# Attention of the first batch pair in whole 128-wide tiles, output stores at another place, and the last addition of the second channel weight's rounding in an adding DMA

## The chip, the core and the metric

The kernel runs on one core of a Trainium2 chip. TensorE (PE) multiplies, VectorE (DVE) and ScalarE (ACT) do elementwise work, GpSimd (POOL) does some too, SyncE (SP) issues most DMAs. The metric is device time in microseconds, lower is better.

## The reference

All inputs are float32 in value; the four MLP weights come in as 8-byte numbers (double precision) and are rounded to float32 on the chip.

```python
kv  = einsum('bhsd,bhse->bhde', k, v)          # 8 batches, 8 heads, s=576, d=64
out = einsum('bhsd,bhde->bhse', q, kv)         # linear attention, no softmax
out = out / sqrt(mean(out*out, -1) + 1e-6) * g_norm
x   = heads side by side                       # (8, 576, 512)
h   = relu(x^T @ w_tok1) @ w_tok2              # token mixing, 576 -> 256 -> 576
u   = x + h^T
out = u + relu(u @ w_ch1) @ w_ch2              # channel mixing, 512 -> 1536 -> 512
```

## The kernel before, in words

A "pair" is two batches (its two "sides"); there are four pairs. The first 200 us are the **front**: attention and token mixing of the pairs, woven with the rounding of the weights. Then comes **channel mixing** for nine groups of 512 rows (eight batches, and the 64 left-over rows of each batch as a ninth), with two nested levels of a seven-product scheme, fed by sums that DVE makes.

The order of the front is written out by hand as lists of step names (`start`, `middle`, `steady`, `last`), which `play` calls one after another. Every instruction is kept in that order on its engine, so a list fixes the order of work on each engine and in each DMA queue. The names: `kvSH` the k^T v products of side S, half H of the heads (into a `ps_kv` bank), `eSH` their copy to `kvp`, `lSH` the load of later k and v, `lqS` the load of q; `aC` the attention product of chunk C (two tiles of 128 rows; chunk 4 is the left-over rows of both sides), `gCh`, `qCh`, `tCh` gain (DVE, L392), square (ACT, L396) and sum of squares (DVE, L412) of one PSUM bank of it, `mC rC iC` mean, square root and a refined reciprocal (L417 to L431), `sCT` and `pCT` the scaling of tile T by ACT (L438, eight small instructions) or by POOL (L443, one instruction). Then `hST` are the first token products, `hr` their remainder with the relu, `uI` the second ones for tile I of nine, `zI` a copy of x into the PSUM bank that `uI` adds to ("seeded" tiles, read back by ACT; the others are added to x by DVE). `jN` are N matmuls of the identity in a stretch with nothing to multiply. `wNK` is step K of rounding token weight block N, `fN` a fetch, a bare number that many further steps of the channel weights' rounding.

Rounding a block (`decode`) is one ACT instruction and then six on DVE: `clamp`, `shift`, `sign`, `power`, `lower`, `both` (in the profile L163, L166, L170, L174, L183, L187, and L118 for `both`, which adds `part` to the block). `part` has one buffer. The second channel weight has six blocks of 128x1024 elements (512 KB each), rounded in the last pair's attention and after it. The first sums of channel mixing read them (`d<-w_ch`, L118).

PSUM in the front: two banks tagged "o" (attention), two "kv", four "h" (token mixing). In `attend` the PE is split into four 64x64 parts; a chunk takes both "o" banks, heads of even number in one and of odd number in the other:

```python
matmul(o[h][ds(n * HF, HF), t, hp],
       lhsT=qT[2 * pair + side][r, hp, ds((2 * (c % 2) + t) * P + n * HF, HF)],
       rhs=kvp[side][r, hp], start=True, stop=True)
```

At the end of the last group, `outer` adds four partial results straight onto the output tile (`put_on`, `write`, `take`, all L118), `xadd` adds the rest, and `store` and `store_rest` (L115) write the 64-row pieces out, half on SP's queue and half on ACT's. The helpers record everything at a few lines: L115 DMA, L118 DVE add, L121 relu, L124 ACT copy, L127 matmul.

Of the kernel before, what the change touches and what calls it, by code (L numbers as in the profile page):

```python
# [19 lines left out]
def kernel(  # L20
# [81 lines left out]
    v_in = [inp.tile([P, JJ, DH], F32, name=f"v_in{i}") for i in range(4)]  # L102
    kvp = [inp.tile([P, HP, D], F32, name=f"kvp{i}") for i in range(2)]
    u_dram = [dram.tile([J * P, DM], F32, name=f"u_dram{g}") for g in range(NG)]
# [43 lines left out]

    def decode(dst, raw):

# [39 lines left out]
        def both():  # L190
            tensor_add(dst, dst, part[0])

# [8 lines left out]

    def block(n, loads, dst):
# [12 lines left out]
        return (fetch,) + decode(dst, turn)  # L215

# [18 lines left out]
    def get_ch2(f):  # L235

        a = 2 * (2 * f // NS)

        def loads(raw):
            t = raw.rearrange("p (h f n) w -> p f h n w", h=2, f=2)  # L240
            rows = words(moe_w_ch2)[ts(f, 2 * P)].rearrange("(f p) (h n) w -> f p h n w", f=2, h=2)
            return [(t[:, i], rows[i]) for i in range(2)]

        dst = w_ch2[:, a:a + 2, ds(2 * f % NS, 2)]
        return block(2 * DM, loads, dst.rearrange("p h f n -> p h (f n)"))

# [84 lines left out]
    def attention(pair, groups):  # L331


        bank, stat, kv_ps = {}, {}, {}

        def kv(side, half):
            n = 4 * pair + 2 * side + half
            kk, vv = k_in[n % 4], v_in[n % 4]

            o = kv_ps[side, half] = ps["kv"].tile([P, 2, D], F32, name="ps_kv")  # L340
            for i in range(2):
                for j in range(JJ):
                    for h in range(2):
                        at = ds(i * P + h * D, D)
                        matmul(o[ds(h * D, D), i], lhsT=kk[:, j, at], rhs=vv[:, j, at],
                               start=(j == 0), stop=(j == JJ - 1), skip_group_check=True)

        def evict(side, half):
            o = kvp[side][:, 2 * half:2 * half + 2]
            if pair == 0:  # L350
                keep(nc.vector.tensor_copy(o, kv_ps[side, half]))
            else:
                copy(o, kv_ps[side, half])

        def attend(c):
            o = [ps["o"].tile([P, 2, HP, D], F32, name="ps_o", tag="o") for _ in range(2)]
            side = c // 2
            for t in range(2):  # L360
                for hp in range(HP):
                    for n in range(2):
                        for h in range(2):
                            r = ds(h * D, D)
                            matmul(o[h][ds(n * HF, HF), t, hp],
                                   lhsT=qT[2 * pair + side][r, hp, ds((2 * (c % 2) + t) * P + n * HF, HF)],
                                   rhs=kvp[side][r, hp], start=True, stop=True)
            for h in range(2):
                bank[c, h] = o[h].rearrange("p t k d -> p (t k) d")

        def attend_rem():
            o = [ps["o"].tile([P, HP, D], F32, name="ps_r", tag="o") for _ in range(2)]
            for hp in range(HP):
                for side in range(2):
                    for h in range(2):
                        r = ds(h * D, D)
                        matmul(o[h][ds(side * HF, HF), hp], lhsT=qT[2 * pair + side][r, hp, LO:],
                               rhs=kvp[side][r, hp], start=True, stop=True)
            for h in range(2):
                bank[4, h] = o[h]  # L380


        number = lambda c: HP if c == 4 else 2 * HP
        sq = {}

        def gain(c, h):
            if (pair, c) not in X:
                n = 1 if c == 4 else 2
                X[pair, c] = xps[pair % 2].tile([P, n, DM], F32, name="x", tag=f"x{n}",
                                                bufs=4 if n == 2 else 1)  # L390
            x = X[pair, c].rearrange("p t (k h d) -> p (t k) h d", h=2, d=D)[:, :, h]
            keep(nc.vector.tensor_mul(x, bank[c, h], g_sb.to_broadcast([P, number(c), D])))  # L392
# [8 lines left out]
        def stats_of(c):  # L401

            g = group(c)
            at = sum(2 * number(i) for i in g if i < c)
            return [t[:, ds(at, 2 * number(c))].rearrange("p (h k) o -> p h k o", h=2) for t in stat[g]]

        def total(c, h):
            g = group(c)
            if g not in stat:
                stat[g] = [stats.tile([P, sum(2 * number(i) for i in g), 1], F32, name=name)  # L410
                           for name in ("ms", "root", "inv")]
# [12 lines left out]
        def invert(g):  # L424
# [6 lines left out]
            keep(nc.vector.reciprocal(inv, root))  # L431

        def scale(c, t):
            x = X[pair, c][:, t].rearrange("p (k h d) -> p k h d", h=2, d=D)
            inv = stats_of(c)[2][:, :, ts(t, HP)]
            for k in range(HP):
                for h in range(2):
                    keep(nc.scalar.activation(x[:, k, h], x[:, k, h], AF.Copy, scale=inv[:, h, k]))  # L438

        def scale_pool(c, t):  # L440
            x = X[pair, c][:, t].rearrange("p (k h d) -> p k h d", h=2, d=D)
            inv = stats_of(c)[2][:, :, ts(t, HP)].rearrange("p h k o -> p k h o")
            keep(nc.gpsimd.tensor_mul(x, x, inv.to_broadcast([P, HP, 2, D])))  # L443

# [6 lines left out]
        for c in range(5):  # L451
            steps[f"a{c}"] = do(attend, c) if c < 4 else attend_rem
            for h in range(2):
                steps |= {f"{n}{c}{h}": do(f, c, h) for n, f in zip("gqt", (gain, square, total))}
# [6 lines left out]

    def token_mixing(pair, seeds):
        h1, acc = {}, {}
# [25 lines left out]
        def tok2(i):  # L489
            if i not in seeds:  # L490
                acc[i] = ps["h"].tile([P, DM], F32, name="ps_u", tag="h")
            first = i not in seeds
# [229 lines left out]
    def outer(place, size, mul, to, base=None, act=copy, onto=False):  # L722
# [56 lines left out]
        at(2, "c", False, True, lambda: take(0, 0, "c", act))  # L779
        put(place + PLACE[7] + 2, do(put_on, 1, 1, "u3"), do(write, 1, 1, "b", "u3"))  # L780
        at(4, "a", False, True, lambda: take(1, 0, "a", copy) if onto else read(to(1, 0), 1, 0))
# [79 lines left out]
    def channel2(g, n0):  # L861
# [104 lines left out]
        else:  # L966
            for place, steps in ((40, [xadd(1, 0, 4)]), (43, [xadd(0, 1, 6)]), (44, [radd(7, 6)]),
                                 (46, [xadd(1, 0, 7)]), (47, [xadd(1, 1, 7)]), (49, [xadd(0, 1, 5)]),
                                 (50, [xadd(1, 1, 5), do(store, g, xg, 1)]),
                                 (52, [do(store_rest, xg, 1)]), (56, [do(store_rest, xg, 0)])):  # L970
# [70 lines left out]
    for t in [t for pair in zip(k_in, v_in) for t in pair]:  # L1041
        keep(nc.gpsimd.memset(t[HF:, J], 0.0))

    root = stats.tile([P, 1], F32, name="root")
# [9 lines left out]
    for block in tok1[2:] + tok2:  # L1054
# [13 lines left out]
    middle = [  # L1068
# [6 lines left out]
    def steady(n0, n1):  # L1075
        return [
            "kv00 l00 e00 1 -s40", "h00 3", "kv01 l01 e01 1", "h01 3", f"a0 q00 g01 q01 g00 {n0}",
# [3 lines left out]
            "u6 t30 t31 m2 r2 1 i2 p20 p21 s30", f"u7 1 s31 {n1}", "u8 2"]  # L1081

    attentions = [attention(0, ((0,), (1,), (2,), (3,), (4,)))]
    attentions += [attention(p, ((0, 1), (2, 3, 4))) for p in range(1, B // 2)]
    mixings = [token_mixing(p, (2, 4, 6) if p < B // 2 - 1 else range(2, 9)) for p in range(B // 2)]
    more = {f"w{n}{k}": f for n, b in enumerate(tok1 + tok2) for k, f in enumerate(b)}
# [13 lines left out]
    for n in range(1, B // 2 - 1):  # L1100
        play(steady(*((2, 0), (2, 1))[n - 1]), attention=attentions[n + 1], mixing=mixings[n], before=attentions[n],
             rounding=rounding)
# [15 lines left out]
    def turn(i):  # L1118
# [6 lines left out]
    last = [  # L1125
        "h00 c0 2 -s40 2", "h01 c1 2", "h10 c2 2", "h11 c3 2", "hr 1", "u0 z2 1", "u1 z3 1", "u2 z4",
        "u3 z5 1", "u4 z6 1", "u5 z7 1", "u6 z8 1", "u7 c4", "u8"]
    more = {f"c{i}": do(turn, i) for i in range(J)}
# [95 lines left out]
```

## Time and profile before

| what | us |
|---|---|
| median of three runs (813.44 to 814.81) | 813.64 |
| the profiled execution: its own time | 815.8 |
| span of its profile | 813.9 |
| PE busy in the span | 786.6 (97%) |
| DVE busy in the span | 681.5 (84%) |
| POOL busy in the span | 77.0 (9%) |

The profiled execution took 2.2 us more than the median of the runs and 1.9 us more than its own span. Busy time is the time in which an engine worked on an instruction. In lists of instructions a line gives start, duration, engine, line, operation, "written <- read", shape, count, and in brackets how long the engine idled before it and what it waited for. One float32 matmul shows as two records on PE.

### The profile page before, as it was taken

The page shows a single profiled execution, that of the slowest core. Times are in us where ns is not written, and L with a number is a line of the kernel's source. Part 1 is how long each engine was busy: PE and PEld are TensorE (multiplying, and loading weights), DVE is VectorE, ACT ScalarE, POOL GpSimd, SP SyncE. Part 2 cuts the span into 40 slices and gives each one's busy share as a digit, 9 for nine tenths or more (in the row PEclk, how much of TensorE's full clock was granted, in tenths as well). Part 3 has the DMA queues.
Part 4 walks back from the last instruction along what each step waited for, and adds up shares of the span by engine and source line. Part 5 has one row for each costly group of instructions (what it writes and reads, how often), then busy time and mean ns, then how long its engine had stood idle before and what let it go on. Part 6 is the DMA issues. An engine that isn't in the chain of part 4 may idle for free.

```text
span 813.9 us, 18057 instructions
## 1 busy us (share of the span) xinstructions
PE 786.6 (97%) x7204; PEld 689.5 (85%) x7204; DVE 681.5 (84%) x1308; ACT 308.1 (38%) x863; POOL 77.0 (9%) x72
## 2 busy tenths in 40 slices
PE   5799999999999999999999999999999999999996
PEld 5445555443788899999999999999999999999996
DVE  3577999999786978987997997897898899799686
ACT  1466667583220034243234233333424323423431
POOL 1100101010000011003003003001100200300300
PEclk9999999999999999999999999999999999999998
DMA  9999999336458567468658638737836855764542
GB/s 286 293 337 294 358 360 347 130 129 178 151 200 274 198 203 242 144 207 233 198 172 255 212 123 279 236 118 230 283 125 213 259 166 196 235 195 147 195 142 82
DMA packets 97348, 175.54 MB, mean 216 GB/s; under 512 B 7024, under 2 KB 54128, under 8 KB 97264
## 3 DMA queue, kind: packets, MB, share of 16 engines
q1 hardware_dynamic: 95584, 172.65, 65.3%
q10 hardware_dynamic: 1680, 1.74, 0.7%
q8 instruction: 57, 0.93, 0.5%
q14 instruction: 27, 0.22, 0.1%
HBM read 137.79 MB, written 36.57 MB: 214 GB/s over the span
## 4 chain that ended last, share of the span: by engine, by line
PE 84%; DVE 8%; DMA 4%; ACT 3%; issue 1%; ACTq 0%; DVEq 0%
PE ps_a L127 37%; PE ps_b L127 18%; PE ps_c L127 9%; PE ps_v L127 4%; PE ps_w L127 4%; PE ps_h L127 4%; PE ps_u L127 4%; ACT x L438 2%; DMA qT<-in_q_dram 1%; DMA v_in<-in_v_dram 1%; PE ps_o L127 1%; DMA k_in<-in_k_dram 1%; DVE ms L412 1%; DVE x L392 1%; PE ps_kv L127 1%
## 5 line engine op out<-in xcount | busy, mean ns | idle before, releaser
L124 ACT COPY u<-ps_a 128x128 f32<-128x128 f32 (+1 forms) x160 | 56.2, 351 | 156.6 <-PE ps_a L127 156.6
L118 POOL TENSOR_TENSOR v<-v,v 128x384 f32<-128x384 f32 (+1 forms) x48 | 61.4, 1300 | 534.4 <-ACT v L124 494.6
L127 PE MATMUL ps_b<-uT,sums 128*128 128x128 f32 x672 | 86.2, 276 | 0.0
L127 PEld LDWEIGHTS ps_b<-uT,sums 128*128 128x128 f32 x672 | 80.7, 192 | 0.2
L118 DVE TENSOR_TENSOR v<-v,v 128x768 f32<-128x768 f32 (+1 forms) x86 | 79.4, 930 | 1.1
L127 PE MATMUL ps_a<-uT,w_ch 128*128 128x128 f32 x576 | 78.8, 275 | 0.0
L124 ACT COPY ps_c<-ps_a 128x128 f32<-128x128 f32 (+1 forms) x80 | 27.0, 337 | 129.5 <-PE ps_a L127 129.5
L127 PE MATMUL ps_u<-h,w_tok 128*128 128x512 f32 (+1 forms) x160 | 69.7, 620 | 3.8 <-DVE w_tok L118 1.9
L118 DVE TENSOR_TENSOR v<-ps_b,u 128x384 f32<-128x384 f32 x112 | 61.3, 547 | 12.7 <-PE ps_b L127 10.8
L127 PEld LDWEIGHTS ps_a<-uT,w_ch 128*128 128x128 f32 x576 | 71.5, 192 | 0.4
L127 PE MATMUL ps_h<-x,w_tok 128*128 128x512 f32 (+1 forms) x160 | 67.3, 612 | 1.5 <-POOL x L443 1.5
L118 DVE TENSOR_TENSOR uT<-uT 128x512 f32<-128x512 f32 (+4 forms) x103 | 63.0, 627 | 0.8
L127 PE MATMUL ps_a<-uT,w 128*128 128x128 f32 x432 | 60.0, 275 | 0.0
L438 ACT ACTIVATE x<-x,inv 128x64 f32<-128x64 f32 x208 | 52.2, 338 | 11.3 <-DVE inv L431 11.3
L127 PEld LDWEIGHTS ps_u<-h,w_tok 128*128 128x128 f32 (+1 forms) x160 | 25.1, 183 | 35.1 <-issue 27.2
L127 PEld LDWEIGHTS ps_a<-uT,w 128*128 128x128 f32 x432 | 54.0, 192 | 0.0
L127 PEld LDWEIGHTS ps_h<-x,w_tok 128*128 128x128 f32 (+1 forms) x160 | 26.0, 190 | 32.3 <-issue 27.2
L121 ACT ACTIVATE v<-v 128x384 f32<-128x384 f32 (+1 forms) x86 | 42.5, 529 | 22.9 <-DVE v L118 22.5
L118 DVE TENSOR_TENSOR xg<-xg,r 128x512 f32<-128x512 f32 x74 | 49.9, 684 | 0.6
L118 DVE TENSOR_TENSOR sv<-v 128x384 f32<-128x384 f32 x80 | 43.3, 550 | 8.0 <-ACT v L121 8.0
L127 PE MATMUL ps_a<-sums,sv 128*128 128x128 f32 x336 | 47.0, 276 | 0.0
L127 PE MATMUL ps_a<-uT,sums 128*128 128x128 f32 x336 | 46.8, 276 | 0.0
(133 smaller groups left out, 1560.2 us busy)
## 6 DMA issues: line engine op xcount, KB each, us to landing
sums<-sums SPq DMA_DIRECT2D x112, 576.0 KB, 4.0
qT<-in_q_dram SPq DMA_DIRECT2D x8, 1152.0 KB, 9.4
xt<-u_dram SPq DMA_DIRECT2D x36, 256.0 KB, 3.7
blocks<-y SPq DMA_DIRECT2D x72, 128.0 KB, 2.6
uT<-blocks SPq DMA_DIRECT2D x36, 256.0 KB, 4.7
xg<-u_dram SPq DMA_DIRECT2D x18, 512.0 KB, 4.8
k_in<-in_k_dram SPq DMA_DIRECT2D x16, 512.0 KB, 9.4
u_dram<-x SPq DMA_DIRECT2D x16, 512.0 KB, 4.9
```

The costliest lines, as they stand in the source:

```text
L118: keep(engine.tensor_tensor(out=o, in0=a, in1=b, op=op))
L121: keep(nc.scalar.activation(o, a, AF.Relu))
L124: keep(nc.scalar.copy(o, a))
L127: keep(nc.tensor.matmul(*a, **kw))
L392: keep(nc.vector.tensor_mul(x, bank[c, h], g_sb.to_broadcast([P, number(c), D])))
L412: keep(nc.vector.tensor_reduce(stats_of(c)[0][:, h], sq[c, h], axis=AX.X, op=ALU.add))
L438: keep(nc.scalar.activation(x[:, k, h], x[:, k, h], AF.Copy, scale=inv[:, h, k]))
```

## The change

1. For pair 0 only (`whole`), the two "kv" banks are zeroed once by DVE and the k^T v products go to the diagonal 64x64 blocks of 128x128 squares. `attend_tile` then multiplies a whole tile of 128 rows by such a square: four 128x128 matmuls per tile in place of 16 of 64x64, into one "o" bank per tile instead of two per chunk. `e` copies 128x256 elements instead of 128x128; gain, square and sum work on one tile each; the left-over rows take one bank. The list `start` is rewritten for it: the tiles `p00 p01 p11 p20 p21 p30 p31` are scaled by POOL and `s10 s40` by ACT (before, ACT scaled one tile of every chunk), `kv11` stands ahead of `h000`, and `j6` and `j2` are added.
2. `both` of the second channel weight's six blocks becomes an accumulating DMA issued by POOL (`part` added to the block in SBUF, 512 KB).
3. In the steady pairs (pairs 2 and 3 of the attention) some scalings are recorded after the matmul or the copy they stood ahead of, and the bare numbers change: three and one more rounding steps in the first of them where there were two and none, none in the second where there were two and one.
4. In the last token mixing, `u0` and `u1` get the "o" banks (free by then), and each seed `z` comes one step earlier.
5. In the last product of the last group, `put_on`/`write` of one quarter come one place earlier; `xadd(1,1,5)` and the store of two pieces move from place 50 to 48, `xadd(0,1,5)` from 49 to 50.

The core of the diff (other hunks only carry `by_dma`, `whole` and the wider `kvp` through):

```diff
...
-    kvp = [inp.tile([P, HP, D], F32, name=f"kvp{i}") for i in range(2)]
+    kvp = [inp.tile([P, HP, P], F32, name=f"kvp{i}") for i in range(2)]
...
         def both():
-            tensor_add(dst, dst, part[0])
+            if by_dma:
+                keep(nc.gpsimd.dma_start(dst, part[0], accum_op=ALU.add))
+            else:
+                tensor_add(dst, dst, part[0])
...
-        return block(2 * DM, loads, dst.rearrange("p h f n -> p h (f n)"))
+        return block(2 * DM, loads, dst.rearrange("p h f n -> p h (f n)"), by_dma=True)
...
+        whole = pair == 0
...
-            o = kv_ps[side, half] = ps["kv"].tile([P, 2, D], F32, name="ps_kv")
+            if whole:
+                o = kv_ps[side, half] = zeroed[half]
+            else:
+                o = kv_ps[side, half] = ps["kv"].tile([P, 2, P], F32, name="ps_kv", tag="kv")
             for i in range(2):
                 for j in range(JJ):
                     for h in range(2):
                         at = ds(i * P + h * D, D)
-                        matmul(o[ds(h * D, D), i], lhsT=kk[:, j, at], rhs=vv[:, j, at],
+                        matmul(o[ds(h * D, D), i, ds(h * D if whole else 0, D)], lhsT=kk[:, j, at],
+                               rhs=vv[:, j, at],
                                start=(j == 0), stop=(j == JJ - 1), skip_group_check=True)
...
-            o = kvp[side][:, 2 * half:2 * half + 2]
-            if pair == 0:
-                keep(nc.vector.tensor_copy(o, kv_ps[side, half]))
+            n = P if whole else D
+            o, i = kvp[side][:, 2 * half:2 * half + 2, :n], kv_ps[side, half][:, :, :n]
+            if whole:
+                keep(nc.vector.tensor_copy(o, i))
             else:
-                copy(o, kv_ps[side, half])
...
+                copy(o, i)
+
+        def attend_tile(c, t):
+            side = c // 2
+            o = ps["o"].tile([P, DM], F32, name="ps_o", tag="o")
+            bank[c, t] = o.rearrange("p (h d) -> p h d", d=D)
+            for hp in range(HP):
+                matmul(o[:, ts(hp, P)], lhsT=qT[2 * pair + side][:, hp, ts(2 * (c % 2) + t, P)],
+                       rhs=kvp[side][:, hp], start=True, stop=True)
+
+        def attend_tile_rem():
+            o = ps["o"].tile([P, DM], F32, name="ps_r", tag="o")
+            bank[4, 0] = o.rearrange("p (h d) -> p h d", d=D)
+            for hp in range(HP):
+                for side in range(2):
+                    matmul(o[ds(side * HF, HF), ts(hp, P)],
+                           lhsT=qT[2 * pair + side][:, hp, LO:],
+                           rhs=kvp[side][:, hp], start=True, stop=True)
...
-                                   rhs=kvp[side][r, hp], start=True, stop=True)
+                                   rhs=kvp[side][r, hp, :D], start=True, stop=True)
...
+        number = lambda c: HP if c == 4 and not whole else H
+        parts = lambda c: 1 if c == 4 and whole else 2
...
-            x = X[pair, c].rearrange("p t (k h d) -> p (t k) h d", h=2, d=D)[:, :, h]
+            if whole:
+                x = X[pair, c][:, h].rearrange("p (h d) -> p h d", d=D)
+            else:
+                x = X[pair, c].rearrange("p t (k h d) -> p (t k) h d", h=2, d=D)[:, :, h]
...
+        def inv_of(c, t):
+
+            inv = stats_of(c)[2]
+            if whole:
+                return inv[:, t].rearrange("p (k h) o -> p k h o", h=2)
+            return inv[:, :, ts(t, HP)].rearrange("p h k o -> p k h o")
...
             x = X[pair, c][:, t].rearrange("p (k h d) -> p k h d", h=2, d=D)
-            inv = stats_of(c)[2][:, :, ts(t, HP)].rearrange("p h k o -> p k h o")
-            keep(nc.gpsimd.tensor_mul(x, x, inv.to_broadcast([P, HP, 2, D])))
+            keep(nc.gpsimd.tensor_mul(x, x, inv_of(c, t).to_broadcast([P, HP, 2, D])))
...
-            steps[f"a{c}"] = do(attend, c) if c < 4 else attend_rem
-            for h in range(2):
+            if whole:
+                steps |= {f"a{c}{t}": do(attend_tile, c, t) if c < 4 else attend_tile_rem
+                          for t in range(parts(c))}
+            else:
+                steps[f"a{c}"] = do(attend, c) if c < 4 else attend_rem
+            for h in range(parts(c)):
                 steps |= {f"{n}{c}{h}": do(f, c, h) for n, f in zip("gqt", (gain, square, total))}
...
             if i not in seeds:
-                acc[i] = ps["h"].tile([P, DM], F32, name="ps_u", tag="h")
+                n = "o" if i in aside else "h"
+                acc[i] = ps[n].tile([P, DM], F32, name="ps_u", tag=n)
...
-        put(place + PLACE[7] + 2, do(put_on, 1, 1, "u3"), do(write, 1, 1, "b", "u3"))
+        put(place + PLACE[7] + (1 if onto else 2), do(put_on, 1, 1, "u3"), do(write, 1, 1, "b", "u3"))
...
         else:
             for place, steps in ((40, [xadd(1, 0, 4)]), (43, [xadd(0, 1, 6)]), (44, [radd(7, 6)]),
-                                 (46, [xadd(1, 0, 7)]), (47, [xadd(1, 1, 7)]), (49, [xadd(0, 1, 5)]),
-                                 (50, [xadd(1, 1, 5), do(store, g, xg, 1)]),
+                                 (46, [xadd(1, 0, 7)]), (47, [xadd(1, 1, 7)]), (48, [xadd(1, 1, 5), do(store, g, xg, 1)]),
+                                 (50, [xadd(0, 1, 5)]),
                                  (52, [do(store_rest, xg, 1)]), (56, [do(store_rest, xg, 0)])):
...
+    zeroed = [ps["kv"].tile([P, 2, P], F32, name="ps_kv", tag="kv") for _ in range(2)]
+    for t in zeroed:
+        keep(nc.vector.memset(t, 0.0))
...
     start = [
         "kv00 e00 l00 j14 w01 w11 w02 w03 w04 w05 w06 w07 w12 w13 w14 w15 w16 w17", "kv01 j10 e01 l01 f0",
-        "a0 q00 g01 q01 g00 t00 t01 m0 r0", "a1 g11 q10 i0 g10 q11 p00 s01 t10 t11 m1 r1",
-        "kv10 e10 i1 p10 s11", "h000 h001", "kv11 e11", "h002 h003",
-        "a2 q20 g21 q21 g20 t20 t21 m2 r2", "h010 h011", "a3 g31 q30 i2 g30 q31 p20 s21 t30 t31 m3 r3",
-        "h012", "a4 i3 p30 s31 q40 g41 q41 g40 t40 t41 m4 r4", "h013 w21 i4 s40 lq0 l10 l11"]
+        "a00 g00 q00", "a01 g01 q01 t00", "a10 g10 q10 t01 m0 r0", "a11 g11 q11 t10 i0 p00 p01",
+        "kv10 j6 t11 m1 r1 e10 i1 s10 p11", "kv11 j2 e11", "h000 h001 h002 h003", "a20 g20 q20", "a21 g21 q21 t20",
+        "h010 t21 m2 r2", "a30 g30 q30 i2 p20", "a31 g31 q31 t30", "h011 t31 m3 r3 p21", "a40 i3 p30 g40 q40 p31",
+        "h012 h013 t40 m4 r4 w21 i4 s40 lq0 l10 l11"]
...
-            "u0 i0 1", "kv11 l11 e11", "u1 1 s00", "u2 z4 1", "a2 q20 g21 q21 g20 s01", "u3 t20 t21",
-            "u4 1 z6", "a4 q40 g41 q41 g40 lq0 s10", "u5 t40 t41 1", "a3 q30 g31 q31 g30 lq1 s11",
-            "u6 t30 t31 m2 r2 1 i2 p20 p21 s30", f"u7 1 s31 {n1}", "u8 2"]
+            "u0 i0 1", "kv11 l11 e11", "u1 1 s00", "u2 z4 1", "a2 q20 g21 q21 g20", "u3 s01 t20 t21",
+            "u4 z6 1", "a4 q40 g41 q41 g40 lq0", "u5 s10 t40 t41 1", "a3 q30 g31 q31 g30 lq1",
+            "u6 s11 t30 t31 m2 r2 1 i2 p20 p21 s30", f"u7 1 s31 {n1}", "u8 2"]
...
-    mixings = [token_mixing(p, (2, 4, 6) if p < B // 2 - 1 else range(2, 9)) for p in range(B // 2)]
+
+    mixings = [token_mixing(p, (2, 4, 6)) for p in range(B // 2 - 1)]
+    mixings.append(token_mixing(B // 2 - 1, range(2, 9), (0, 1)))
...
-        play(steady(*((2, 0), (2, 1))[n - 1]), attention=attentions[n + 1], mixing=mixings[n], before=attentions[n],
+        play(steady(*((3, 1), (0, 0))[n - 1]), attention=attentions[n + 1], mixing=mixings[n], before=attentions[n],
...
-        "h00 c0 2 -s40 2", "h01 c1 2", "h10 c2 2", "h11 c3 2", "hr 1", "u0 z2 1", "u1 z3 1", "u2 z4",
-        "u3 z5 1", "u4 z6 1", "u5 z7 1", "u6 z8 1", "u7 c4", "u8"]
+        "h00 c0 2 -s40 2", "h01 c1 2", "h10 c2 2", "h11 c3 2", "hr z2 1", "u0 z3 1", "u1 z4 1", "u2 z5",
+        "u3 z6 1", "u4 z7 1", "u5 z8 1", "u6 1", "u7 c4", "u8"]
```

More of the change, by code (lines that the diff above doesn't have):

```diff
@@ L146, in load_q, with decode @@
             dma(qT[b], q[b].rearrange("(c p) s -> p c s", p=P))
-    def decode(dst, raw):
+    def decode(dst, raw, by_dma=False):
         bits = dst.bitcast(U32)
@@ L200, in like, with block @@
         return flat if len(dst.shape) == 2 else flat.rearrange("p (a n) -> p a n", a=dst.shape[1])
-    def block(n, loads, dst):
+    def block(n, loads, dst, by_dma=False):
         raw = []
@@ L213, in turn @@
             return t if len(dst.shape) == 2 else t.rearrange("p (a n) w -> p a n w", a=dst.shape[1])
-        return (fetch,) + decode(dst, turn)
+        return (fetch,) + decode(dst, turn, by_dma)
     def get_tok1(t):
@@ L377, in attend_rem @@
                         matmul(o[h][ds(side * HF, HF), hp], lhsT=qT[2 * pair + side][r, hp, LO:],
-                               rhs=kvp[side][r, hp], start=True, stop=True)
+                               rhs=kvp[side][r, hp, :D], start=True, stop=True)
             for h in range(2):
                 bank[4, h] = o[h]
-        number = lambda c: HP if c == 4 else 2 * HP
+        number = lambda c: HP if c == 4 and not whole else H
+        parts = lambda c: 1 if c == 4 and whole else 2
         sq = {}
@@ L403, in stats_of @@
             g = group(c)
-            at = sum(2 * number(i) for i in g if i < c)
-            return [t[:, ds(at, 2 * number(c))].rearrange("p (h k) o -> p h k o", h=2) for t in stat[g]]
+            n = lambda i: parts(i) * number(i)
+            at = sum(n(i) for i in g if i < c)
+            return [t[:, ds(at, n(c))].rearrange("p (h k) o -> p h k o", h=parts(c)) for t in stat[g]]
         def total(c, h):
@@ L409, in total @@
             if g not in stat:
-                stat[g] = [stats.tile([P, sum(2 * number(i) for i in g), 1], F32, name=name)
+                stat[g] = [stats.tile([P, sum(parts(i) * number(i) for i in g), 1], F32, name=name)
                            for name in ("ms", "root", "inv")]
@@ L431, in invert @@
             keep(nc.vector.reciprocal(inv, root))
+        def inv_of(c, t):
[3 more added lines that the diff above has]
+            return inv[:, :, ts(t, HP)].rearrange("p h k o -> p k h o")
         def scale(c, t):
             x = X[pair, c][:, t].rearrange("p (k h d) -> p k h d", h=2, d=D)
-            inv = stats_of(c)[2][:, :, ts(t, HP)]
+            inv = inv_of(c, t)
             for k in range(HP):
                 for h in range(2):
-                    keep(nc.scalar.activation(x[:, k, h], x[:, k, h], AF.Copy, scale=inv[:, h, k]))
+                    keep(nc.scalar.activation(x[:, k, h], x[:, k, h], AF.Copy, scale=inv[:, k, h]))
         def scale_pool(c, t):
             x = X[pair, c][:, t].rearrange("p (k h d) -> p k h d", h=2, d=D)
-            inv = stats_of(c)[2][:, :, ts(t, HP)].rearrange("p h k o -> p k h o")
-            keep(nc.gpsimd.tensor_mul(x, x, inv.to_broadcast([P, HP, 2, D])))
+            keep(nc.gpsimd.tensor_mul(x, x, inv_of(c, t).to_broadcast([P, HP, 2, D])))
         steps = {}
@@ L459, in attention, with token_mixing @@
         return steps
-    def token_mixing(pair, seeds):
+    def token_mixing(pair, seeds, aside=()):
         h1, acc = {}, {}
```

## The prediction

> **What bounds the kernel now.** I read the busy time by stage first, then the chain of work that ended last, then PE's own list for its gaps. By stage (columns: stretch, length, busy time and count of PE, PE's weight loads, DVE, ACT, POOL, then granted clock, DMA share, GB/s):
>
> ```profile
> 31.00:59.00 28.00, 23.22 (x339) 12.68 (x340) 18.90 (x46) 14.09 (x43) 2.12 (x2) 0.93 1.07 323
> 85.00:128.00 43.00, 42.74 (x527) 22.15 (x523) 39.64 (x69) 28.92 (x88) 2.79 (x2) 1.00 1.07 363
> 128.00:173.50 45.50, 43.56 (x530) 22.25 (x526) 43.53 (x67) 29.78 (x87) 2.79 (x2) 1.00 0.54 197
> 206.60:805.00 598.40, 598.40 (x5025) 588.64 (x5026) 508.84 (x1009) 190.73 (x523) 61.39 (x48) 1.00 0.61 199
> ```
>
> From 206.6 to 805 PE has no gap, so no edit can gain there; a gain has to be made in the front or the last 9 us, and every us that PE starts 206.6 sooner is a us off the end. The chain (start, length, what) shows what holds the front:
>
> ```profile
> 19.64 11.20 DMA qT<-in_q_dram
> ...
> 35.25 2.86 issue
> ...
> 48.12 2.03 ACT x L438 x8
> ...
> 58.66 4.52 PE ps_u L127 x6
> ...
> 206.59 36.46 PE ps_v L127 x168
> ```
>
> Up to 30.84 DMA sets the pace, then pair 0's second half runs through small DVE and ACT steps with a 2.86 us PE wait that no semaphore explains, then the rounding of w_tok2 ends at 58.5 and lets `u0` go. PE's gaps:
>
> ```profile
> 38.11 0.30 PE L127 MATMUL ps_o<-kvp,qT 64*64 64x64 f32 x2 [2.86 <-issue]
> 58.66 4.51 PE L127 MATMUL ps_u<-h,w_tok 128*128 128x512 f32 x6 [1.92 <-DVE w_tok L118]
> ...
> 160.88 1.98 PE L127 MATMUL ps_u<-h,w_tok 128*128 128x512 f32 x4 [0.74 <-ACT ps_u L124]
> 166.91 1.16 PE L127 MATMUL ps_o<-kvp,qT 64*64 64x64 f32 x64 [1.12 <-ACT sq L396]
> 197.58 9.00 PE L127 MATMUL ps_u<-h,w_tok 128*128 128x512 f32 x24 [1.10 <-ACT ps_u L124]
> ```
>
> The tail, DVE's last rows and the store:
>
> ```profile
> 806.53 0.29 DVE L118 TENSOR_TENSOR xg<-ps_b,xg 128x128 f32<-128x128 f32 x1
> ...
> 807.92 0.29 DVE L118 TENSOR_TENSOR xg<-ps_b,xg 128x128 f32<-128x128 f32 x1
> ```
>
> **What the Trainium skill says.** (1) "DMA: Bandwidth & Descriptors", section "SWDGE vs HWDGE vs iDMA": accumulating is possible only in DMAs issued from GpSimd, whose descriptors a program on GpSimd writes; "Anatomy of one DMA — SWDGE (gpsimd) path" prices one at 2.0 us + bytes / 436e3. No such DMA is in this trace. (2) "SBUF — State Buffer", section "Who interferes with whom": a DVE instruction in a two-port mode locks GpSimd out, descriptor writing included. The trace has contention of that kind: an L118 `w_ch` add of 128x768, else 0.96 us, took 1.70 us where POOL was scaling. (3) "Runtime: NRT & Kernel Launch", section "Instruction fetch mechanics": instructions come in blocks of 256 by a DMA, mostly hidden. The 2.86 us "issue" gap, in the middle of 64 tiny records while the DMA engines are full, looks like one that wasn't; the trace doesn't name it.
>
> **1, pair 0 by whole tiles.** PE: a tile is 4 matmuls = 8 records; 12 records of 128x128 take 1.34 us, so 0.89 us, and a chunk 1.8 instead of 1.16. Nine tiles cost 8.0 us for about 6.2; PE has gaps here, so this 1.8 costs little. `e`: a 128x256 PSUM read takes 0.42 for 0.28, four times +0.14, hidden before 30 us. What it gives is that a gain starts after one tile and an "o" bank returns when its tile is read.
>
> I laid the new list out by hand with the row durations: gain and sum 0.63, square 0.60, `m` 0.17, root 0.22, `i` 0.87, POOL scale 1.06, `h` 0.95, kv 1.31. The first tile starts at 18.4 as before; `i0` ends at 25.2 and POOL has x0 at 26.3 (before 25.4), x1 at 27.3. `kv11` now stands ahead of `h000` and needs v that was issued at 16.2 to 18.7 and lands 9 to 10 us later, about 27; so `h003` ends at 32.5 and `a20` runs then, not at 30.97. That is 1.5 us given away. From there: tiles 32.5 to 34.3, `t21` to 36.3, `i2` to 38.0, `t31` 39.9, `i3` 41.2, `g40` 41.8, `t40` 43.1, `i4` 44.4. Before, `i4` ended at 48.09. The w_tok2 rounding behind it takes 10.5 us (48.0 to 58.5), so it ends at 54.9. PE meanwhile: `kv00` 40.6, `h10` (x7 scaled by POOL at 43.4) to 45.5, `kv01` (its v lands about 44.5) to 46.9, `h11`, `hr`, `a0` to 53.6, first half of `u0` 54.5. So `u0` goes on at 54.9 for 58.66: **-3.7 us**. The 2.86 gap goes with it: 104 fewer matmuls for the same work ask for instructions more slowly. If the gap recurs elsewhere, the gain is about 1.5; if `kv11` doesn't wait, 5.2. Later loads are no bar: q of the next pair lands at 49.4 (issued 41.75, 7.6 to landing) and is needed at 52.5; k and v needed at 61.6 were issued by 50.3 and land within 10 us.
>
> **2, the adding DMA.** It takes six DVE adds of 1.22 us off, 7.3 in all, three in pair 3 and three after. It adds six DMAs in POOL's queue: behind them wait POOL's `p20 p21` of pair 3 only, needed 10 us later. The new wait is DVE's: `power` of the next block writes the one `part` and waits for the DMA. Everything of DVE stands behind it. Latency L: at least 2.0 + 524288/436e3 = 3.2 (estimate from page 1); 512 KB weight loads at that place took 4.5 to landing, plus 1.4 of `clamp` and `shift` (0.68 + 0.69) that may keep POOL from writing descriptors: I take **L = 6**; upper end 9, as the k and v loads in full DMA traffic (9.4).
>
> Block 0 to 1 in pair 3 is the tight place: only 2.6 us of `clamp`, `shift`, `sign` between. From the gain of `a0` (138.98): 1.28 + power 0.69 + sums 1.27 + `lower` 1.21 = 143.4; + 6 = 149.4; power, `lower` 1.92: the gain of `a1` starts at 151.3 for 152.24. Two further steps now lie ahead (1.9 us, edit 3); DVE's waits in pair 2 (0.19 + 0.69 + 0.92 + 0.57) take most, say 0.6 is left. Net +0.3 us of the 0.74 gap; at L = 3.2 both gaps there go (+1.9), at L = 9 -2.3. The next blocks have over 7 us between. After pair 3, block 4 to 5 has 3.9 us, so 2.1 of stall, but three adds are gone (3.7): nothing. The first `d<-w_ch` that needs block 5 has 6.9 us.
>
> **3, moved scalings.** On ACT they keep their place but for one copy that now precedes `s10`/`s11`; order on PE is unchanged. The added step in pair 2 brings an ACT rounding read ahead of the relu of `hr`; its load, issued at 96.07, lands at 104.5, so the relus end 1.3 us later, and squares behind them about 0.5. **+0.4 us** lost (0 to 1.5).
>
> **4, u0 and u1 in "o".** The 1.10 gap at 197.58 is ACT's seed waiting for a DVE add (196.25) to free an "h" bank. Those banks are no longer taken: **-1.1 us**. Next late is uT's sums (in before at 204.96; first needed 1.8 us into ps_v): not late.
>
> **5, tail.** The last product waits 0.24 us for the `write` at 806.53; that comes at 805.96. DVE's last add then ends near 807.8 for 808.21. Each queue issues its four stores one after another from 807.45, 2.47 us in SP's queue and 2.75 in ACT's, so the fourth starts near 809.4; with the first two gone at 805.8 it starts at 808.0. **-1.3 us** (0.4 if only PE's gap counts, 1.5).
>
> Sum: 3.7 + 0.3 - 0.4 + 1.1 + 1.3 = 6.0. The profiled execution's 815.8 becomes 809.8; against the median, 813.64 - 6.0 = **807.6**.
>
> **Rivals.** (A) The start is held by DMA or by another instruction gap: part 1 gives 1.0, sum 3.3, 810.3. For it: DMA share 1.07 from 24 to 140. Against: no PE wait for DMA after 30.84. (B) No `kv11` wait and a short L: 5.2 + 1.5 - 0.4 + 1.1 + 1.3 = 8.7, 804.9. (C) The other side: the adding DMA is slow. Beyond L = 6 pair 3 loses 1 us per us; from 8.6 uT's sums lose it again. At L = 12: pair 3 -4.9, later -3.4, sum 3.7 - 0.4 - 4.9 - 3.4 + 1.1 + 1.3 = -2.6, 816.2; it decides from L about 10.7. For it: L is in no row here, and a two-port lock can hold POOL. Against: DMA share is only 0.54 there. (D) What is gained is absorbed by a later wait of the front, such as ACT's squares at 166.9: 813.
>
> **How the numbers follow.** Chances: forecast (805.8 to 809.4) 0.53, A 0.18, B 0.15, C 0.08, D 0.06. Range 803.8 to 811.8. A difference under 0.2%, 1.6 us, can't be told from none. Faster by more: 0.53 + 0.15 + most of A, 0.85; within 0.08; slower 0.07.
>
> **What would show it.** Right: `u0` of pair 0 complete near 55; no "issue" gap at 35; `power` in pair 3 waiting for a POOL DMA some 3 us once; the PE gap at 197 gone; the last stores issued by 808.7. Wrong: `kv11` or `kv01` waiting for v longer than here, a `part` wait over 6 us, or new gaps in PE between 60 and 200.

## The result, and the profile after

The changed kernel takes as long as the kernel before: 814.54 us (median of four runs, 813.81 to 814.89) against 814.11 (four runs, 813.44 to 814.81); ratio 1.0004, 95% interval 0.9987 to 1.0021. The forecast was 807.6 us.

The change did most of what it was forecast to do, and gave it all back in one place. The same stages as shown of before, in the profile of the changed kernel (same columns; this execution took 813.81 us, the least of its four, and its span is 812.0, 1.9 us less than that of before, though the medians agree):

```profile
31.00:59.00 28.00, 27.27 (x300) 15.62 (x299) 23.07 (x51) 12.69 (x30) 4.08 (x4) 1.00 1.08 343
85.00:128.00 43.00, 41.88 (x489) 21.21 (x488) 38.98 (x66) 28.66 (x90) 2.39 (x2) 1.00 1.07 361
128.00:173.50 45.50, 39.83 (x477) 20.29 (x478) 34.12 (x54) 25.54 (x70) 4.13 (x3) 0.96 0.68 194
206.60:805.00 598.40, 598.33 (x5026) 588.57 (x5025) 509.14 (x1010) 190.03 (x523) 61.40 (x48) 1.00 0.63 199
```

The first stage got 4 us fuller on PE (27.27 busy for 23.22). The third, the last pair's attention, got emptier: 39.83 for 43.56 on PE, and DVE fell from 43.53 to 34.12. DVE has three adds less there (3.7 us), and it stood for 11.4 us of this stretch, for 2.0 before; 9.2 of the 11.4 are two waits that its own list will show. The last row is as full as before, so for it only its beginning counts: `ps_v` starts at 206.25, for 206.52 before.

PE's own list tells where the lead was lost (start, duration, work, and in brackets the idle time ahead and what ended it):

```profile
54.48 2.81 PE L127 MATMUL ps_u<-h,w_tok 128*128 128x512 f32 x6 [0.55 <-DVE w_tok L118]
...
143.28 1.16 PE L127 MATMUL ps_o<-kvp,qT 64*64 64x64 f32 x64
...
153.86 0.46 PE L127 MATMUL ps_o<-kvp,qT 64*64 64x64 f32 x16 [1.25 <-ACT kvp L124]
156.09 1.07 PE L127 MATMUL ps_o<-kvp,qT 64*64 64x64 f32 x48 [1.77 <-ACT kvp L124]
...
160.98 1.98 PE L127 MATMUL ps_u<-h,w_tok 128*128 128x512 f32 x4 [0.40 <-ACT ps_u L124]
164.39 0.70 PE L127 MATMUL ps_r<-kvp,qT 64*64 64x64 f32 x32 [1.43 <-ACT sq L428]
```

`u0` goes on at 54.48 for 58.66, and no PE wait in the start is named "issue" any more. At `a1` of the last pair (143.28) PE is 4.5 us ahead of the kernel before (147.80). At `u4`, 160.98, it is 0.1 us behind (160.88). The profile of before carries some 1.7 us of its own that other profiles of the old start lack (see part 1 below), so the lead is smaller than it looks: e8, with the old start, has `a1` at 146.35 and `ps_v` at 205.05. In between PE waits for ACT, and ACT for DVE. DVE's list of those 20 us, where `power` is L183, `lower` L187 and the gain L424:

```profile
139.00 1.22 DVE L187 SCALAR_TENSOR_TENSOR part<-raw,part 128x1024 f32<-128x1024 uint32 x1
...
150.47 0.69 DVE L183 TENSOR_SCALAR part<-w_ch 128x1024 uint32<-128x1024 uint32 x1 [7.66 <-DMA w_ch<-part]
151.20 1.23 DVE L187 SCALAR_TENSOR_TENSOR part<-raw,part 128x1024 f32<-128x1024 uint32 x1
152.34 1.28 DVE L424 TENSOR_TENSOR x<-ps_o,g_sb 128x512 f32<-128x512 f32 x2
...
161.09 0.69 DVE L183 TENSOR_SCALAR part<-w_ch 128x1024 uint32<-128x1024 uint32 x1 [1.50 <-DMA w_ch<-part]
```

The second block's `power` waits 7.66 us for the first block's adding DMA to let go of `part`; the gain of `a1` stands behind it and starts at 152.34. In the kernel before it started at 152.24, as the rows of before show (PE's `a1`, then DVE's gain of it, L392 there):

```profile
147.80 1.16 PE L127 MATMUL ps_o<-kvp,qT 64*64 64x64 f32 x64
...
152.24 1.28 DVE L392 TENSOR_TENSOR x<-ps_o,g_sb 128x512 f32<-128x512 f32 x2
```

The forecast allowed 6 us from the end of `lower` to `power`; it took 10.2. The chain of waits now has that DMA in it, which it had not before. The second block below is from the list of DMA issues of the 3 us around it (KB each, us from issue to landing):

```profile
140.53 9.84 DMA w_ch<-part
```

```profile
raw<-in_moe_w_ch_dram SPq DMA_DIRECT2D x2, 512.0 KB, 5.0
w_ch<-part POOLq DMA_DIRECT2D x1, 512.0 KB, 9.8
```

These two lines are the clue: `lower`, whose end releases the adding DMA, is also the last reader of a `raw` buffer, and SP at once issues a later block's load into it, two DMAs of 512 KB. From issue to landing the six adding DMAs took 9.8, 8.3, 5.0, 5.8, 6.1 and 5.5 us; weight loads go beside the first two alone (other, smaller or later DMAs run beside the rest). In all DVE waits 12.0 us for them (7.66 + 1.50 + 2.85), for 7.3 us of adds saved.

The tail came sooner by 1.6 us (start of `ps_v` to the end of the span, 607.38 before, 605.75 now). SP's queue of output stores starts at 807.45 in the kernel before, at 805.70 now:

```profile
807.45 2.47 SPq L115 DMA_DIRECT2D out_dram<-xg  x4
```

```profile
805.70 2.96 SPq L115 DMA_DIRECT2D out_dram<-xg  x4
```

### The profile page after: what moved, and what is told of

The parts are those of the page before. It is cut to its first block, busy times and chain, and to the rows that moved or that the text cites. A ratio compares the mean times of both kernels' runs of the same rounds, so it can differ in the third digit from the quotient of the medians.

```text
span 812.0 us, 17668 instructions
## 1 busy us (share of the span) xinstructions
PE 789.2 (97%) x7012; PEld 693.9 (85%) x7012; DVE 676.2 (83%) x1302; ACT 301.8 (37%) x838; POOL 87.4 (11%) x81
## 4 chain that ended last, share of the span: by engine, by line
PE 82%; DVE 7%; DMA 5%; ACT 4%; issue 1%; SPq 0%; DVEq 0%; ACTq 0%
PE ps_a L127 37%; PE ps_b L127 19%; PE ps_c L127 9%; PE ps_v L127 4%; PE ps_w L127 4%; PE ps_u L127 4%; PE ps_h L127 3%; DMA v_in<-in_v_dram 2%; ACT x L478 2%; DVE x L424 1%; DMA w_ch<-part 1%; DVE ms L445 1%; DMA raw<-in_moe_w_ch_dram 1%; DMA k_in<-in_k_dram 1%; PE ps_o L127 1%
## 5 line engine op out<-in xcount | busy, mean ns | idle before, releaser
L118 DVE TENSOR_TENSOR v<-ps_b,u 128x384 f32<-128x384 f32 x112 | 61.5, 549 | 12.9 <-PE ps_b L127 11.2
L478 ACT ACTIVATE x<-x,inv 128x64 f32<-128x64 f32 x184 | 46.0, 336 | 9.6 <-DVE inv L464 9.6
```

The source lines that it names most:

```text
L118: keep(engine.tensor_tensor(out=o, in0=a, in1=b, op=op))
```

## The experiments

**Theory**: the adding DMA is slow where loads run beside it, `power` waits for `part`, and that wait eats what parts 1, 4 and 5 gain. **Rivals**: the start's gain is absorbed by a later wait of the last pair anyway; or the DMA costs through its traffic or through what reads the block, not through the buffer; or the adding itself is what is slow. Ratios are to the kernel before, timed on the same chip, with their 95% intervals.

| kernel | median us | ratio |
|---|---|---|
| as changed | 814.54 | 1.0004 (0.9987 to 1.0021) |
| e3, part 1 alone | 810.46 | 0.9957 (0.9939 to 0.9974) |
| e4, part 2 alone | 822.22 | 1.0105 (1.0089 to 1.0121) |
| e7, part 4 alone | 811.96 | 0.9974 (0.9960 to 0.9987) |
| e8, part 5 alone | 811.81 | 0.9967 (0.9957 to 0.9978) |
| e9, parts 1, 4, 5 | 806.83 | 0.9917 (0.9903 to 0.9931) |
| e1, all but part 2 | 806.77 | 0.9917 (0.9902 to 0.9931) |
| e2, all, second block's part elsewhere | 806.38 | 0.9912 (0.9896 to 0.9928) |
| e10, as e2, old rounding numbers | 807.42 | 0.9923 (0.9910 to 0.9936) |
| e5, all, without two loads | 807.69 | 0.9920 (0.9903 to 0.9937) |
| e6, all, copy in place of adding | 810.14 (one run) | none |
| e11, all, filler matmuls | 814.89 | 1.0013 (1.0007 to 1.0019) |

**e3, part 1 alone.** The changed kernel with parts 2 to 5 taken back. 

> The kernel before with part 1 alone (first pair by whole tiles, its list of steps). Theory (the start's gain of 4 to 6 us lasts to the end when nothing takes it): 808 to 810.5. Rival (a later wait of the front absorbs it): 812.5 to 814.5.

 Measured: 0.9957 of 813.69 is 3.5 us less (2.1 to 5.0). The start's gain lasts to the end when nothing takes it.

**e4, part 2 alone**, put into the kernel before:

```diff
-            tensor_add(dst, dst, part[0])
+            if by_dma:
+                keep(nc.gpsimd.dma_start(dst, part[0], accum_op=ALU.add))
...
```

> The kernel before with part 2 alone (the six additions by the adding DMA). Theory (10 us from issue to landing at the first block): a DVE wait of 5 to 8 us at the second block's power in the last pair's attention, less the adds saved: 816 to 820, 2 to 6 us slower than before. Rival (the DMA is harmless without the new start, since pair 3 comes later): within 1.5 us of before, about 814.

 Measured: 8.5 us slower (7.2 to 9.8), beyond the range of both. In its DVE list `power` waits four times, not three:

```profile
153.60 0.69 DVE L183 TENSOR_SCALAR part<-w_ch 128x1024 uint32<-128x1024 uint32 x1 [7.91 <-DMA w_ch<-part]
...
164.69 0.69 DVE L183 TENSOR_SCALAR part<-w_ch 128x1024 uint32<-128x1024 uint32 x1 [1.97 <-DMA w_ch<-part]
...
191.28 0.69 DVE L183 TENSOR_SCALAR part<-w_ch 128x1024 uint32<-128x1024 uint32 x1 [3.81 <-DMA w_ch<-part]
...
208.47 0.69 DVE L183 TENSOR_SCALAR part<-w_ch 128x1024 uint32<-128x1024 uint32 x1 [3.07 <-DMA w_ch<-part]
```

They sum to 16.8 us; less the 7.3 us of adds that is 9.4, near the 8.5 measured. So the wait isn't a product of the new start.

**e1, all but part 2.** The adds are DVE's again:

```diff
-    return block(2 * DM, loads, dst.rearrange("p h f n -> p h (f n)"), by_dma=True)
+    return block(2 * DM, loads, dst.rearrange("p h f n -> p h (f n)"))
```

> The changed kernel with one part undone: the six last additions of the second channel weight are DVE adds again, all else stays changed. Theory (the waits of DVE for the adding DMA, 7.66 + 1.50 + 2.85 = 12.0 us against 7.3 us of adds, eat what the start gained): PE enters the last stretch (ps_v at 206.25 in the changed kernel) 4 to 6 us sooner, and the time is 807 to 810. Rival (what the start gains is absorbed in the last pair's attention by DVE's and ACT's own work, whoever adds): within 1.5 us of the changed kernel, 813 to 815.5.

 Measured: 806.77, just under the theory's range, and `ps_v` at 199.31, 6.9 us sooner than in the changed kernel, where 4 to 6 were expected. Part 2 costs the changed kernel 1.0004 - 0.9917 = 0.87% of 814, about 7.1 us. The rival of absorption falls.

**e2, the buffer alone.** The adding DMAs stay; the second block's `part` lies in a k buffer that nothing needs any more:

```diff
-    flat = stage.tile([P, 2 * DM], F32, name="part", tag="part", bufs=1)
+    flat = stage.tile([P, 2 * DM], F32, name="part", tag="part", bufs=1) if room is None else room
...
+    room=k_in[0].rearrange("p j e -> p (j e)") if f == 1 else None
```

> The changed kernel with the adding DMAs kept, but the second block's part in other memory (a k buffer that is dead by then), so that its power step needn't wait for the first block's DMA. Theory (it is the wait on the one part buffer that costs): the 7.66 us wait at 150 is gone, a smaller one may come for the third block, and the time is 3.5 to 6.5 us less than the changed kernel's, 808 to 811. Rival (the DMA costs by its traffic, by POOL or by what reads the block, not by the buffer): less than 1.5 us gained.

 Measured: 806.38, by the ratios 0.92% or 7.5 us less than the changed kernel, more than expected. The profile of e2, DVE's list at the same place:

```profile
138.48 1.21 DVE L187 SCALAR_TENSOR_TENSOR part<-raw,part 128x1024 f32<-128x1024 uint32 x1
...
142.31 0.69 DVE L183 TENSOR_SCALAR k_in<-w_ch 128x1024 uint32<-128x1024 uint32 x1
```

No wait, and the first adding DMA still takes 10.0 us to land, the second 9.9. So at this place the latency by itself costs nothing; only the one buffer turns it into a wait. The later `power` of e2 still waits 2.79 us at 192.86, and PE has no gap between 161 and `ps_v` (198.47): that wait is covered. The expected wait of the third block didn't come. And by the times e2 can't be told from e1: six adds off DVE buy nothing that these runs resolve, though `ps_v` comes 0.8 us sooner in e2's profile (198.47 for 199.31). DVE had time to spare after it in both: it waits for PE 4.09 us at 202.30, and 3.32 in e1.

**e5, the loads beside it.** The kernel leaves out the loads of the last two blocks:

```diff
...
+            if f in (4, 5):
+                raw.append(raws[f - 4])
+                return
             raw.append(stage.tile([P, n, 2], U32, name="raw", tag="raw", bufs=4))
...
```

> The changed kernel without the loads of the fifth and sixth block of the second channel weight (2 MB, which start together with the first and the second adding DMA); those two blocks are rounded again from the first two blocks' raw words instead, so their values are left out. Theory (an adding DMA takes 5 to 6 us by itself, and 8.3 to 9.8 only beside 1 MB of loads): issue to landing of the first two falls to 5 to 6.5 us, the wait at the second block's power from 7.66 to 3 to 4.5 us, and the time by 2.5 to 5 us against the changed kernel. Rival (the first two are slow for another reason, such as DVE's steps beside them): still 8 to 10 us to landing, the wait above 6.

 Measured: 807.69, 6.8 us less than the changed kernel, more than expected. In e5's profile, the adding DMA of the first block, then DVE's row of the second block's `power`:

```profile
w_ch<-part POOLq DMA_DIRECT2D x1, 512.0 KB, 5.1
```

```profile
144.80 0.69 DVE L183 TENSOR_SCALAR part<-w_ch 128x1024 uint32<-128x1024 uint32 x1 [2.98 <-DMA w_ch<-part]
```

It lands in 5.1 us for 9.8, the second in 5.4 for 8.3. The 2.98 us wait that is left shows in no PE gap near it: PE has none from 112 to 155. That is the wait the forecast had priced, "some 3 us once", and it costs nothing that can be measured (e5 0.9920, e1 0.9917; forecast was a gain of 0.3 us).

**e6, copy or add.** The addition is left out:

```diff
-    keep(nc.gpsimd.dma_start(dst, part[0], accum_op=ALU.add))
+    keep(nc.gpsimd.dma_start(dst, part[0]))
```

> The changed kernel with a plain DMA copy by POOL in place of the adding one (the addition is left out; bytes written, issuer and order are the same). If the adding itself is what takes long: to landing under 6 us for the first block and a wait under 4. If it is the loads beside it: still 8 to 10 us for the first two blocks and 4.5 to 6 for the others, as in the changed kernel.

 Measured: between the two. To landing 7.3 and 5.8 us beside the weight loads (adding: 9.8 and 8.3), and 3.1, 4.8, 3.6 and 4.3 us for the later blocks, without them (adding: 5.0, 5.8, 6.1 and 5.5). POOL was busy 0.74 us (median) with one, 1.24 with an adding one. So the adding costs 1 to 2.5 us, block by block, and the loads beside it 3 to 5 us more (e5). The `power` wait fell to 5.12 us. One run only; its profile has no low clock at that place.

**e7, part 4 alone**, in the kernel before; the seeds `z` move one place with it:

```diff
-    acc[i] = ps["h"].tile([P, DM], F32, name="ps_u", tag="h")
+    n = "o" if i in aside else "h"
+    acc[i] = ps[n].tile([P, DM], F32, name="ps_u", tag=n)
...
```

> The kernel before with part 4 alone (u0 and u1 of the last token mixing in the attention's banks, seeds one step earlier). Forecast of it: the 1.10 us gap of PE at 197.58 is gone and nothing else moves: 1.1 us faster. Rival: the gap is another wait's cover (uT's sums), and nothing is gained.

 Measured: 2.1 us less (1.1 to 3.3). The 1.10 us gap is gone; from `a3` of the last pair to `ps_v` it takes 38.23 us (164.86 to 203.09) against 39.60 in e8 (165.45 to 205.05), which still has the gap: 1.4 us by the traces.

**e8, part 5 alone**, in the kernel before:

```diff
-        put(place + PLACE[7] + 2, do(put_on, 1, 1, "u3"), do(write, 1, 1, "b", "u3"))
+        put(place + PLACE[7] + (1 if onto else 2), do(put_on, 1, 1, "u3"), do(write, 1, 1, "b", "u3"))
...
-    (49, [xadd(0, 1, 5)]),
-    (50, [xadd(1, 1, 5), do(store, g, xg, 1)]),
+    (48, [xadd(1, 1, 5), do(store, g, xg, 1)]),
+    (50, [xadd(0, 1, 5)]),
```

> The kernel before with part 5 alone (two of the last stores sooner). Forecast of it: from the start of ps_v to the end of the span 1.3 to 1.6 us less, the time 1.3 us faster (0.4 if only PE's own gap counts).

 Measured: 2.7 us less (1.8 to 3.5). From `ps_v` to the end of the span its profile has 605.55 us for 607.38, 1.8 us less.

**e9, parts 1, 4 and 5.** e1 with the steady pairs' lists of before. 

> Parts 1, 4 and 5 alone: DVE adds as before, and the steady pairs' lists as before (no part 3). Forecast of part 3: it loses 0.4 us (0 to 1.5), so this would be 0.4 us faster than the kernel with parts 1, 3, 4 and 5 (ratio 0.9917 of before), about 806.4, with no 7 us wait of ACT for a load ahead of the relus near 100. Rival (part 3 gains, since it takes ACT's scalings out of the way of copies): 1 to 2.5 us slower than that kernel, 808 to 809.5.

 Measured: the same ratio as e1. Part 3 costs or gains nothing that can be measured. In the changed kernel's profile it does what was forecast: ACT's read of a raw block waits 7.97 us for its load ahead of the relus, and PE 0.85 us at 101.96 behind it. In e1's profile ACT waits 6.97 us and PE not at all.

**e10, e2 with the old numbers** of rounding steps:

```diff
-    play(steady(*((3, 1), (0, 0))[n - 1]), ...
+    play(steady(*((2, 0), (2, 1))[n - 1]), ...
```

> The changed kernel with the second block's part in other memory, and the rounding steps of the steady pairs at their old numbers (two and none, two and one). If the early step costs (ACT's 7 us wait for a load ahead of the relus): 0.3 to 1 us faster than with the other memory alone (ratio 0.9912 of before), about 805.5 to 806.2. If the old numbers bring the last pair's rounding back among its attention and DVE is late there: as fast or up to 2 us slower.

 Measured: 807.42, 1.0 us more than e2. That lies within the second expectation and not the first, but the intervals of the two runs overlap, so a difference is not shown. The lateness is not where it was expected either: the last block is rounded later, its adding DMA takes 10.6 us to land beside loads of channel mixing (`xg`, `xt`), and a sum that reads the block (`d<-w_ch`) waits 3.72 us for it at 208.62.

**e11, the low clock.** After PE's gaps at 154 and 156 its granted clock is low. Windows of 2 us of the changed kernel:

```profile
154.00:156.00 2.00, 0.33 (x16) 0.19 (x14) 1.97 (x5) 0.34 (x2) 0.33 (x1) 1.00 0.85 284
156.00:158.00 2.00, 1.91 (x49) 1.39 (x50) 1.90 (x7) 0.09 (x2) 0.00 (x0) 0.68 0.93 268
158.00:160.00 2.00, 2.00 (x4) 0.67 (x2) 1.59 (x2) 2.00 (x9) 0.00 (x0) 0.50 1.10 204
```

The edit puts `j`, 14 matmuls of the identity, ahead of `a2` in the last pair:

```diff
-    "u2 z4 1", "a2 q20 g21 q21 g20", ...
+    "u2 z4 1", *(("j",) if n0 == 0 else ()), "a2 q20 g21 q21 g20", ...
...
```

> The changed kernel with 14 matmuls of the identity (28 records of 128x128, about 3.1 us, nothing reads them) ahead of the third chunk's attention product of the last pair, where PE idles 1.25 and 1.77 us behind the adding DMA's wait and its granted clock is then 0.50 to 0.68 for about 4 us. DVE's waits are not touched. Theory (the idle brings the low clock, which costs PE some 1.7 us more): the clock stays 1.00 from 150 to 174 and the time is 1 to 2 us less than the changed kernel's, about 813. Rival (the low clock comes with the place or the load, not with the idle): the same dip, and the time the same or up to 1 us more.

 Measured: 814.89, no gain. The same windows of e11:

```profile
154.00:156.00 2.00, 1.96 (x17) 1.96 (x18) 1.97 (x5) 0.16 (x2) 0.51 (x1) 1.00 0.90 303
156.00:158.00 2.00, 2.00 (x54) 1.88 (x57) 1.90 (x6) 0.22 (x2) 0.00 (x0) 1.00 1.05 270
158.00:160.00 2.00, 2.00 (x40) 1.06 (x32) 1.77 (x3) 1.86 (x8) 0.00 (x0) 1.00 1.02 194
```

The clock stays at 1.00 with the idle filled, so the low clock came with the idle; but the time doesn't follow. PE waits longer afterwards (1.93 us for ACT's square at 165.07, for 1.43): at this place PE follows DVE and ACT, and a slow PE costs nothing that can be measured.

## Why the prediction was wrong, step by step

**The step that failed is part 2's latency, "I take L = 6".** Measured at that place: 10.2 us from the end of `lower` to `power`, 9.84 from issue to landing. The value was built from 512 KB loads that "took 4.5 to landing" there, plus 1.4, and for the loads 4.5 was about right (5.0 here). What it left out is that the same `lower` releases such loads, 1 MB of them, which run beside the adding DMA: e5 takes them away and finds 5.1. The stage's mean DMA share of 0.54, used against rival C, can't show two bursts that meet. The upper bound of 9 was too low as well.

The rest of that step was right: at 5 to 6 us it costs nothing that can be measured (e5), and the first half of rival C, a slow adding DMA that holds up pair 3, is what happened. C was to decide "from L about 10.7"; 9.8 was enough. It was given 8%. Its second half, late sums of uT, did not happen here.

**What the longer latency cost was under-sized too.** By the forecast's rule (1 us per us) 3.8 us more latency turn +0.3 into -3.5; its own figures for L = 9 and 12, -2.3 and -4.9, are even 0.4 and 0.8 below that rule. Against e1, `ps_v` comes 6.9 us later in the changed kernel. The first 0.8 is there before the DMA is issued (`a1` of the last pair at 143.28 for 142.44): it is PE's wait at 101.96, behind part 3. The other 6.1 can be read from DVE's gains in the last pair. In e1 those of `a0` and `a1` stand at

```profile
135.17 1.28 DVE L424 TENSOR_TENSOR x<-ps_o,g_sb 128x512 f32<-128x512 f32 x2
...
146.39 1.28 DVE L424 TENSOR_TENSOR x<-ps_o,g_sb 128x512 f32<-128x512 f32 x2
```

that is 11.2 us apart; in the changed kernel it is 16.3 (136.01 to 152.34), 5.1 more. The forecast compared with the list of before, where it is 13.3 (138.98 to 152.24): it credited the DMA with the two rounding steps that part 3 takes out of this stretch, but in e1 they are out of it too. The gain of `a2` comes another 1.6 us later (162.96 for 155.42). 1.50 of that is a second wait that the forecast had excluded ("the next blocks have over 7 us between"): they had 7.2 us, but with loads beside it that DMA took 8.3. Of these 6.7 us, 6.1 arrive at `ps_v`; the low clock is not needed to explain them, and e11 shows no gain without it.

**Part 1, 3.7 us: right.** 3.5 (2.1 to 5.0) in e3. The traces of before and after differ by 5.9 us at `a0` of pair 2 (94.47 and 88.57), because the profiled execution of before had a second stretch of low clock (0.50 to 0.67 from 58 to 62), which cost it about 1.7: the six records of `u0` at 58.66 took 4.51 us there and 2.81 in the changed kernel. e7 and e8, with the old start, are free of that one. A detail was wrong: v landed at 25.7, not 27, so `a20` ran at 31.34 for the 32.5 forecast. The "issue" gap of 2.6 to 2.9 us stands in all four profiles of the old start and in none of the nine of the new one. Its cause stays open. With it went a stretch of low clock that the forecast hadn't named: the mean clock was 0.991 to 0.996 in all executions of before timed beside the experiments and 0.997 to 0.999 in those of e3. How much of the 3.5 us that is, no run separates.

**Part 3, -0.4 (0 to 1.5): within its bounds**, 0 by e1 and e9. The wait came where it was forecast, and cost PE 0.85 us in the changed kernel's profile and nothing in e1's.

**Part 4, +1.1: right in kind**, 1.4 by the traces, 2.1 (1.1 to 3.3) by the times.

**Part 5, +1.3: too small**, 1.8 by the traces and 2.7 (1.8 to 3.5) by the times. The forecast stopped at the start of the fourth store. The end of the span comes 5.98 us after DVE's last add begins in the kernel before (807.92 to 813.9) and 4.23 in e8 (806.37 to 810.6); over all profiles it is 5.8 to 6.0 without part 5 (before, e3, e4, e7) and 4.1 to 4.4 with it, so 1.4 to 1.9 us are shown by the traces.

**The sum.** Parts 1, 4 and 5 were forecast at 6.1 us; e9 measures 6.8 (5.6 to 7.9). The three measured alone add up to 8.3, so what the times of e7 and e8 show beyond their traces may be scatter; that stays open. Had part 2 cost nothing, as in e2, the forecast of 807.6 would have been 1.2 us from the time. Rivals A (the start held by DMA) and D (absorbed later) are refuted by e3 and e1.

**What the Trainium skill said.** The price in "DMA: Bandwidth & Descriptors", section "Anatomy of one DMA — SWDGE (gpsimd) path", gives 3.2 us for this size (an estimate from it). e6's plain copy took 3.1 for the third block, which agrees, and 3.6 to 4.8 for the later ones. An adding one took 5.0 to 6.1 without weight loads beside it, in the changed kernel and in e5: there the measurement decides, and the price is short by 2 to 3 us. The 1.4 us that the forecast added for a DVE lock on POOL isn't there: POOL's six issues took 1.19 to 1.60 us in the changed kernel, and `clamp` or `shift` ran beside four of them (1.21 to 1.60), so it is 0.4 at most. The add of 1.70 us that the forecast took for contention of that kind is neither of these two instructions and showed nothing of them. L = 6 was near for an undisturbed DMA, but of other parts than thought. The skill has a word on the low clock too: "TensorE: Matmul & The Clock Gate", section "🔬 Part 1: The HAM clock gate (the "warmup" mystery)", says that PE's clock is halved after an idle window of some 3.4 us, at windows that run free of the kernel. The 0.50 agrees with the half; but here it came after single gaps from 1.92 us up, shorter than that.

## What to carry to other kernels

When a DVE operation is handed to a DMA, ask what frees its source buffer and who writes it next: with one buffer, the latency becomes a wait of the engine that was to be relieved. Price that latency beside everything that the same step issues, loads of later blocks above all, and not by a stage's mean DMA share. And moving work off an engine need not pay even when its new place is hidden: e2 keeps PE free of waits for the adding DMA, and its times can't be told from those of e1.

## What the runs showed of the hardware

An adding DMA of 512 KB inside SBUF, issued by POOL, took 5.1 and 5.4 us to land with no SP or ACT DMA beside it (e5) and 5.0 to 7.2 beside other DMAs than weight loads. Beside weight loads of 1 MB or more it took 8.3 to 10.3, and once 10.6 beside channel mixing's loads (e10). A plain copy took 3.1 to 4.8 without the weight loads and 5.8 to 7.3 beside them (e6). An adding one kept POOL busy for 1.2 to 1.6 us, a copy for 0.7 to 1.2.

A short idle of PE can halve its clock, for 3.4 or 6.8 us in each case seen: after the 2.6 to 2.9 us "issue" gap in all four profiles of the old start (before, e4, e7, e8), after 1.92 us once (before, 58.66), and with a pair of gaps with little between in e4 and the changed kernel. Not after 1.93 us in e11, 2.04 in e6 or 2.61 at 203.80 in e4, nor after the 1.3 us gap that all profiles have between 72 and 80. So the length of a gap alone doesn't decide; what does wasn't tried.
